# An mLSTM and bilinear layer in one launch: the order of its instructions is planned with other durations, a shared port, other rates of transfers and a model of the clock

## The chip, the cores and the metric

One core of one Trainium2 chip runs the whole program. TensorE is PE here, VectorE DVE, ScalarE ACT, GpSimd POOL, and SyncE, which issues every DMA, SP. The metric is the device time of one execution in microseconds; the shown time is the median of the runs.

## What is computed

An mLSTM over 768 positions for 4 batches and 8 heads of width 40 gives y. Its 3072 rows of 320 then go through a bilinear layer with 1536 hidden columns:

```python
for t in range(S):
    m_new = np.maximum(f + m, i)
    f_stab, i_stab = np.exp(f + m - m_new), np.exp(i - m_new)
    C = f_stab * C + i_stab * outer(v, k)
    n = f_stab * n + i_stab * k
    y = sigmoid(o) * (C @ q) / np.maximum(np.abs(n @ q), 1.0)
x = y as (3072, 320)                    # q, k, v, gates: float32
out = ((x @ w_a) * (x @ w_b)) @ w_out   # w_a, w_b, w_out: float64
```

## The kernel before

The positions are cut into 6 chunks of 128 for each of 4 batches: 24 chunks n, each for all heads. Of a chunk, in this order: `qk` and `va` are loaded; T holds the transposed q (`T<n>_0`) and k (`T<n>_1`); `pS` = k q; the masked weights of the gates are in `gbc<n>` (POOL masks them by affine_select, ACT takes eight exponentials, one for each head, from chunk 4 on); DVE multiplies `pS` with `gbc`; `pI` is q times the state of the chunks before; `pV` is the weighted sum of v; `pU` adds `vw` (v weighed by POOL with columns of `gtab`) times k to the state `cst`; `num`, `den` and `osig` make y; `pX` transposes y into `xh` (cast by ACT) and its rest `xl` (subtracted by DVE). Chunks from 6 on split their operands into bf16 parts: `r`, the `qks` tiles, and `pb`, `vr`, `vl`, `cr`, `cb`.

The columns of all gates, `gtab`, are transposed once (`ptg`), and exponentiated once on ACT, in a table of functions other than that of the sigmoid that makes `osig`.

The 24 chunks are grouped into 9 blocks of 2 or 3 for the bilinear layer. For each ff of 12, `pu<block>_<ff>_0` and `_1` are 8 matmuls each (xh and xl with the high and low parts of w_a and w_b); ACT or DVE copies the first into `g`, DVE multiplies the second into it, `gh` and `gl` are its two parts, and two ff later `pd<block>_<chunk>` gets three matmuls of each chunk. While block kb runs, the chunks of block kb+1 go through the attention, so their instructions lie between those of the block.

The float64 weights come in 32 pieces (`raw0` to `raw31`) and are converted on chip, one after the other, during blocks 0 and 1: two ACT steps (into `qks`, used as scratch, and `cw`), one DVE step on `cw`, a cast `w` on ACT and its rest `w` on DVE. A piece must be done before the matmuls that read it.

No instruction is issued where it is written. Every call goes into a `Plan`, which keeps for each node its engine, a duration `occ`, a delay `lat` until others see it, and its dependences; buffers are rings, so the first user of a slot depends on the last of the tile before. `settle` then lists the nodes: `run` takes, engine by engine, the ready node with the best rank, and ranks are found by running the plan backwards, 6 turns. Nodes that are marked as pinned (the start up to the first weights) keep their written order on an engine. The best plan's order is written out engine by engine, and semaphores keep the dependences on the chip. `HOP` is what a signal between engines takes. The instructions written by `emit` all have the line of its call.

Of the kernel before, what the change touches and what calls it, by code (L numbers as in the profile page):

```python
# [21 lines left out]
TURNS = 6  # L22
LANES = 8


# [74 lines left out]
class Node:  # L100
    __slots__ = (
        "i", "eng", "calls", "occ", "lat", "prev", "next", "table", "acc", "pinned", "at", "done", "xfer",
    )

    def __init__(self, i, eng):
        self.i, self.eng, self.calls, self.prev, self.next = i, eng, [], {}, []
        self.occ = self.lat = self.xfer = 0.0
        self.table, self.acc, self.pinned = None, [], False


class Plan:

    ENGINES = {"tensor": "PE", "vector": "DVE", "scalar": "ACT", "gpsimd": "POOL", "sync": "SP"}
    HOP = 0.07

    def __init__(self, nc):
        self.nc, self.nodes, self.rings, self.pinned = nc, [], {}, True
        for name in self.ENGINES:  # L120
            setattr(self, name, Recorder(self, name))

    def pool(self, pool, space, bufs):
        return Pool(self, pool, space, bufs)

    def add(self, engine, op, args, kw):
        eng = self.ENGINES[engine]
# [12 lines left out]
        if not (  # L140
            eng == "PE" and node is not None and node.eng == "PE" and node.acc[0][0] == okey
            and len(node.calls) < 8 and node.pinned == self.pinned
        ):
            node = Node(len(self.nodes), eng)
            node.pinned = self.pinned
            self.nodes.append(node)
        node.calls.append((engine, op, args, kw))
        node.acc += acc
        self.cost(node, eng, op, out, refs, args, kw)
        return Issued()  # L150
# [15 lines left out]

    def cost(self, node, eng, op, out, refs, args, kw):
        cols = int(np.prod(out.shape[1:]))
        size = [x.size if isinstance(x, View) else mybir.dt.size(x.dtype) for x in refs]
        if eng == "PE":  # L170
# [12 lines left out]
        elif eng == "ACT":  # L183
            func = str(args[2]) if op == "activation" else "Copy"
            node.table = "S" if "Sigmoid" in func else "E" if "Exp" in func else None
            bias = hasattr(kw.get("bias"), "shape")
            node.occ = 0.04 + cols * 0.00094 + (0.13 if bias else 0.0)
            node.occ += 0.05 if "Prelu" in func or "scale" in kw else 0.0
            node.lat = 0.11
        elif eng == "DVE":  # L190
            rate = 960.0
            one = op in ("tensor_copy", "tensor_scalar", "memset") and all(
                not isinstance(x, View) or x.root.ring[0] != "psum" for x in refs
            )
# [4 lines left out]
            node.occ = 0.065 + cols / rate  # L199
            node.lat = 0.085  # L200
        elif eng == "POOL":
            node.occ = 0.1 + cols * (0.0009 if op in ("affine_select", "memset") else 0.002)
            node.lat = 0.1
        elif op == "dma_start_transpose":
            node.occ, node.lat, node.xfer = 1.3, 1.6, 0.0
        else:
            n = int(np.prod(out.shape)) * size[0]
            rows = out.shape[-1] * size[0]
            node.occ, node.lat = 0.47 if rows > 512 else 0.6, 1.7
            node.xfer = n / (340e3 if rows > 512 else 172e3)  # L210

# [35 lines left out]
    def edge(self, a, b, order=False):  # L247
        if a is b or (order and a.i in b.prev):
            return
        if a.eng == b.eng and a.eng != "SP":  # L250
            gap = a.occ
            if a.eng in ("DVE", "ACT", "POOL") and not order:
                gap += 0.06
        else:
            gap = a.occ if order else None
        if order and a.eng != b.eng:
            gap = 0.0
        if a.i not in b.prev:
            a.next.append(b)
            b.prev[a.i] = gap  # L260
        elif gap is None or (b.prev[a.i] is not None and gap > b.prev[a.i]):
            b.prev[a.i] = gap

    def run(self, rank, forward=True):
        nodes = self.nodes
# [6 lines left out]
        end = [0.0] * len(nodes)  # L272
        table, wire, landed = "E", 0.0, []
        order = []
        for x in nodes:
            if lack[x.i] == 0:
                heapq.heappush(wait[x.eng], (0.0, rank[x.i], x.i))
        while len(order) < len(nodes):
            best = None
            for e in engines:  # L280
                if ready[e]:
                    t = free[e]
                elif wait[e]:
                    t = max(free[e], wait[e][0][0])
                else:
                    continue
                if best is None or t < best[0]:
                    best = (t, e)
            t, e = best
            while wait[e] and wait[e][0][0] <= t + 1e-9:  # L290
                r, k, i = heapq.heappop(wait[e])
                heapq.heappush(ready[e], (k, i))
            k, i = heapq.heappop(ready[e])
            x = nodes[i]
            if x.table and x.table != table:
                table = x.table
                t += 1.283
            at[i] = t
            free[e] = t + x.occ
            if e == "SP":  # L300
                if forward:
                    if len(landed) >= LANES:
                        t = max(t, landed[-LANES])
                    at[i], free[e] = t, t + x.occ
                    wire = max(wire, t + x.lat) + x.xfer if x.xfer else wire
                    end[i] = wire + 0.35 if x.xfer else t + x.occ + x.lat
                    landed.append(end[i])
                else:
                    free[e] = t + max(x.occ, x.xfer)
                    end[i] = t + x.occ + x.lat + x.xfer  # L310
            else:
                end[i] = t + x.occ + x.lat
            order.append(x)
            for y in x.next if forward else [nodes[j] for j in x.prev]:
                lack[y.i] -= 1
                if lack[y.i] == 0:
                    r = 0.0
                    if forward:
                        for j, gap in y.prev.items():
                            r = max(r, end[j] + self.HOP if gap is None else at[j] + gap)  # L320
                    else:
                        for z in y.next:
                            gap = z.prev[y.i]
                            r = max(r, at[z.i] + z.occ + (y.lat + self.HOP if gap is None else gap - y.occ))
                    heapq.heappush(wait[y.eng], (r, rank[y.i], y.i))
        return order, at, max(end)

    def settle(self):
# [3 lines left out]
        for turn in range(TURNS):  # L332
            order, at, end = self.run(rank)
            if best is None or end < best[1]:
                best = (order, end, at)
            back, late, _ = self.run([-t for t in at], forward=False)
            rank = [-(t + x.occ) for t, x in zip(late, self.nodes)]
        self.at = best[2]
# [3 lines left out]
    def emit(self, order):  # L342
# [3 lines left out]
        for node in order:  # L346
            for engine, op, args, kw in node.calls:
                f = getattr(getattr(self.nc, engine), op)
                f(*[real(x) for x in args], **{k: real(x) for k, x in kw.items()})  # L349
# [6 lines left out]
class Recorder:  # L356

    def __init__(self, plan, name):
        self._plan, self._name = plan, name

    def __getattr__(self, op):
        return lambda *args, **kw: self._plan.add(self._name, op, args, kw)

# [1058 lines left out]
```

## Time and profile before

| what | value |
|---|---|
| median of 3 runs | 553.07 us (552.47 to 554.78) |
| profiled execution, its own time | 552.61 us |
| its span, first to last instruction | 550.8 us |
| PE busy | 529.5 us, 96% |
| DVE, ACT, POOL busy | 408.0, 234.4, 126.1 us |
| mean granted clock of PE | 0.966 |

Busy time is what an engine works, waits are idle time before an instruction with the one that released it, and the granted clock says which share of the full rate PE had. All rows have line 349, the call in `emit`, so that the names of the tiles tell the steps apart; buffer numbers are left out in the rows, so `T` is any T and `gbc` any gbc.

### The profile page before, as it was taken

The page shows a single profiled execution, that of the slowest core. Times are in us where ns is not written, and L with a number is a line of the kernel's source. Part 1 is how long each engine was busy: PE and PEld are TensorE (multiplying, and loading weights), DVE is VectorE, ACT ScalarE, POOL GpSimd, SP SyncE. Part 2 cuts the span into 40 slices and gives each one's busy share as a digit, 9 for nine tenths or more (in the row PEclk, how much of TensorE's full clock was granted, in tenths as well). Part 3 has the DMA queues.
Part 4 walks back from the last instruction along what each step waited for, and adds up shares of the span by engine and source line. Part 5 has one row for each costly group of instructions (what it writes and reads, how often), then busy time and mean ns, then how long its engine had stood idle before and what let it go on. Part 6 is the DMA issues. An engine that isn't in the chain of part 4 may idle for free. (4 is left out here: it accounts for less than half of the span.)

```text
span 550.8 us, 12384 instructions
## 1 busy us (share of the span) xinstructions
PE 529.5 (96%) x4810; PEld 506.3 (92%) x4810; DVE 408.0 (74%) x940; ACT 234.4 (43%) x556; POOL 126.1 (23%) x185
## 2 busy tenths in 40 slices
PE   7787899989999999999999999999999999999997
PEld 5676899989999999999899999999999999999997
DVE  5897875578969985987869985988869856844342
ACT  5689997354523642432623444432432622311111
POOL 2012353453232231242132131232030202000000
PEclk9668799989999999999999999999999999999999
DMA  9999923559767756479745659567635535100001
GB/s 170 304 255 312 163 54 65 150 87 166 149 142 125 159 121 149 96 123 171 134 118 129 100 131 191 91 137 147 120 107 86 115 64 116 38 1 26 1 1 37
DMA packets 198679, 66.77 MB, mean 121 GB/s; under 512 B 184252, under 2 KB 191900, under 8 KB 198620
## 3 DMA queue, kind: packets, MB, share of 16 engines
q1 hardware_dynamic: 198620, 65.98, 58.1%
q8 instruction: 38, 0.62, 0.5%
q14 instruction: 21, 0.17, 0.1%
HBM read 41.11 MB, written 5.97 MB: 85 GB/s over the span
## 5 line engine op out<-in xcount | busy, mean ns | idle before, releaser
L349 PE MATMUL pu<-xh,w 128*128 128x384 f32 (+1 forms) x1080 | 281.5, 328 | 0.6 <-ACT xh L349 0.6
L349 PE MATMUL pu<-xl,w 128*128 128x384 f32 (+1 forms) x648 | 211.9, 329 | 1.0 <-DVE xl L349 1.0
L349 PEld LDWEIGHTS pu<-xh,w 128*128 128x128 f32 x1080 | 195.6, 194 | 1.7 <-ACT xh L349 1.0
L349 PE MATMUL pd<-w,gh 128*128 128x320 f32 x576 | 134.5, 315 | 0.0
L349 PEld LDWEIGHTS pu<-xl,w 128*128 128x128 f32 x648 | 126.0, 194 | 2.1 <-DVE xl L349 1.3
L349 PEld LDWEIGHTS pd<-w,gh 128*128 128x128 f32 x576 | 98.0, 190 | 0.4
L349 DVE TENSOR_TENSOR g<-pu,g 128x384 f32<-128x384 f32 (+1 forms) x108 | 54.7, 507 | 57.9 <-PE pu L349 53.5
L349 PE MATMUL pd<-w,gl 128*128 128x320 f32 x288 | 90.4, 315 | 0.0
L349 ACT COPY g<-pu 128x384 f32<-128x384 f32 (+1 forms) x92 | 40.3, 438 | 96.5 <-PE pu L349 96.3
L349 ACT ACTIVATE gbc<-gbc,gtab 128x128 f32<-128x128 f32 x160 | 54.3, 394 | 20.5 <-POOL gbc L349 20.5
L349 POOL TENSOR_TENSOR vr<-va 128x336 f32<-128x336 f32 x18 | 14.5, 804 | 211.7 <-PE pV L349 211.7
L349 PEld LDWEIGHTS pd<-w,gl 128*128 128x128 f32 x288 | 54.3, 189 | 0.2 <-DVE gl L349 0.2
L349 DVE TENSOR_TENSOR gl<-g,gh 128x384 fp32r<-128x384 f32 (+1 forms) x92 | 51.7, 562 | 1.9
L349 ACT CAST pb<-gbc 128x512 bf16<-128x512 f32 x36 | 22.3, 619 | 45.0 <-DVE gbc L349 44.8
L349 PE MATMUL pV<-va,gbc 128*128 128x42 bf16 (+1 forms) x240 | 36.2, 235 | 1.8 <-ACT T L349 1.8
L349 DVE CAST gh<-g 128x384 fp32r<-128x384 f32 (+1 forms) x96 | 33.9, 353 | 1.7
L349 DVE TENSOR_TENSOR num<-pV,num 128x336 f32<-128x336 f32 x20 | 10.1, 505 | 32.9 <-PE pV L349 32.9
L349 DVE TENSOR_TENSOR gbc<-pS,gbc 128x512 f32<-128x512 f32 x48 | 32.3, 680 | 2.9 <-PE pS L349 2.3
L349 ACT CAST cb<-cst 128x168 bf16<-128x168 f32 x18 | 6.0, 333 | 61.6 <-DVE cst L349 34.2
L349 PE MATMUL pS<-T,T 120*128 120x128 bf16 (+1 forms) x352 | 29.4, 236 | 1.8 <-DVE T L349 1.8
L349 PEld LDWEIGHTS <-T 120*128 120x128 bf16 x576 | 24.7, 97 | 6.4 <-issue 4.1
L349 POOL TENSOR_TENSOR gl<-g,gh 128x256 fp32r<-128x256 f32 x16 | 13.1, 821 | 56.5 <-ACT gh L349 49.7
(102 smaller groups left out, 763.7 us busy)
## 6 DMA issues: line engine op xcount, KB each, us to landing
gbc<-g_dram SPq DMA_DIRECT2D x20, 512.0 KB
qk<-in_q_dram SPq DMA_DIRECT2D x24, 160.0 KB
qk<-in_k_dram SPq DMA_DIRECT2D x24, 160.0 KB
va<-in_v_dram SPq DMA_DIRECT2D x24, 160.0 KB
osig<-in_o_gate_dram SPq DMA_DIRECT2D x24, 160.0 KB
raw<-in_moe_w_out_dram SPq DMA_DIRECT2D x12, 320.0 KB
out_dram<-o SPq DMA_DIRECT2D x24, 160.0 KB
raw<-in_moe_w_a_dram SPq DMA_DIRECT2D x8, 384.0 KB
```

Of the source, the lines that this page charges most:

```text
L349: f(*[real(x) for x in args], **{k: real(x) for k, x in kw.items()})
```

## The change

Only the planner changes. The durations of most kinds of instructions are set anew, as is HOP; a step after another on the same engine that reads its result costs `DEP`. DVE and POOL exclude each other in the plan where both use the SBUF port that they share (`port`). The plan of PE counts the columns and rows that it uses in a window of `SPELL` us, and doubles the duration of matmuls where the window before was used under 0.375. Transfers are slower (305 and 160 KB per us in place of 340 and 172), a long one lands 1.2 us later in the plan, and of those with short rows no more than two are on the way at a time. Nodes may have several engines to choose from (`alts`, `copier`, `adder`), but no call uses that: every instruction keeps its engine, and the instructions of each engine are the same as before. The core of the diff:

```diff
+SPELL = 3.4133
...
-    HOP = 0.07
+    HOP = 0.05
+    DEP = {"DVE": 0.115, "ACT": 0.115, "POOL": 0.11, "PE": 0.0}
...
                 elif "float32r" in f32[0]:
-                    occ = cols / 2400 + 0.011
+                    occ = cols / 2400 + 0.0135
                 else:
-                    occ = 0.108 if refs[1].shape[0] <= 64 else 0.22
-            node.occ += occ
-            node.lat = 0.17
+                    occ = 0.108 if cols > 64 else 0.052
+            by[0] += occ
+            by[1] = 0.17
+            plain = size[1] == 4 and op == "matmul" and "float32r" not in f32[0]
+            node.use += cols * refs[1].shape[0] * (1 + plain) / 128.0 * out.shape[0] / 128.0
...
-            node.occ = 0.1 + cols * (0.0009 if op in ("affine_select", "memset") else 0.002)
-            node.lat = 0.1
+            by[0] = 0.03 + cols * 0.00205
+            if op == "affine_select":
+                by[0] = 0.05 + cols * 0.001
+            elif op == "memset":
+                by[0] = 0.05 + cols * 0.0008
+            by[1] = 0.06
+            by[3] = op != "memset"
...
-            node.xfer = n / (340e3 if rows > 512 else 172e3)
+            by[2] = n / (305e3 if node.wide else 160e3)
...
+            if shared and forward:
+                t = max(t, port[other[e]])
+                port[e] = t + occ - 0.07
+            if e == "PE" and forward:
+                w = int(t / SPELL)
+                if used.get(w - 1, 0.0) < 0.375 * SPELL * 2400:
+                    occ = 2 * occ
+                used[w] = used.get(w, 0.0) + x.use
...
+                    if not x.wide:
+                        if len(slim) > 1:
+                            free[e] = max(free[e], slim[-2] - 0.3)
-                    end[i] = wire + 0.35 if x.xfer else t + x.occ + x.lat
+                    end[i] = wire + (1.2 if x.wide and xfer > 1.0 else 0.35) if xfer else t + occ + lat
```

The order changes most in blocks 0 and 1 (until about 150 us) and a little after. Three places follow.

ACT ahead of the exponential of `gtab`, some 46 to 50 us into the span (w10 to w12, cw and qks are conversion steps of the weights, gh0_2 a part of block 0). Before:

```order
L349 CAST w10_648<-cw_582 128x384
L349 ACTIVATE qks1_87<-raw13_398 128x320
L349 ACTIVATE cw_659<-raw13_398 128x320
L349 CAST w11_667<-cw_616 128x384
L349 CAST gh0_2_676<-g0_2_588 128x256
L349 ACT_TABLE_LOAD
L349 ACTIVATE osig0_218<-osig0_218 128x2x320
L349 ACT_TABLE_LOAD
L349 ACTIVATE gtab_105<-gtab_105 128x5x64
L349 ACTIVATE dec_106<-pdec_687 128x64
L349 CAST w12_706<-cw_639 64x384 x2
```

Now:

```order
L420 ACTIVATE qks1_87<-raw13_388 128x320
L420 ACT_TABLE_LOAD
L420 ACTIVATE osig0_237<-osig0_237 128x2x320
L420 CAST w10_659<-cw_575 128x384
L420 ACT_TABLE_LOAD
L420 ACTIVATE gtab_105<-gtab_105 128x5x64
L420 ACTIVATE dec_106<-pdec_650 128x64
L420 CAST gh0_2_677<-g0_2_583 128x256
L420 CAST w11_682<-cw_607 128x384
L420 ACTIVATE cw_688<-raw13_388 128x320
L420 CAST w12_702<-cw_625 64x384 x2
```

The cast of w11, gh0_2 and the second step on raw13 stood ahead of gtab and now stand behind it; osig0 and its table load come earlier.

PE around `pI5`, the product of chunk 5 with the state before it, in block 1 at 113 to 119 us. Before, from the end of pu1_4_1 and pU5 on:

```order
L349 MATMUL pu1_4_1_1592<-xh1_999,w12_706 128x256
L349 MATMUL pU5_1606<-vw5_1458,qk2_82 64x42 x8
L349 MATMUL pI5_0_1626<-cst1_91,T5_0_1400 128x42 x2
L349 MATMUL pI5_1_1630<-cst1_91,T5_0_1400 128x42 x2
L349 MATMUL pI5_0_1626<-cst1_91,T5_0_1400 128x42
L349 MATMUL pI5_1_1630<-cst1_91,T5_0_1400 128x42
L349 MATMUL pI5_0_1626<-cst1_91,T5_0_1400 128x42
L349 MATMUL pI5_1_1630<-cst1_91,T5_0_1400 128x42
L349 MATMUL pu1_4_1_1592<-xl1_1016,w12_706 128x256
L349 MATMUL pd1_0_1518<-w7_529,gh1_2_1529 128x320 x2
```

Now pU5 stands 26 rows ahead of the first of pI5 (one row of pu1_4_1, the downs of ff 2 and all of pu1_5 follow it); the last of these, and pI5:

```order
L420 MATMUL pu1_5_1_1635<-xl1_1011,w11_682 128x256
L420 MATMUL pu1_5_1_1635<-xh1_1000,w11_682 128x256
L420 MATMUL pu1_5_1_1635<-xh1_1000,w12_702 128x256
L420 MATMUL pu1_5_1_1635<-xl1_1011,w12_702 128x256
L420 MATMUL pd1_0_1521<-w13_733,gh1_3_1565 128x320 x2
L420 MATMUL pd1_0_1521<-w13_733,gl1_3_1571 128x320
L420 MATMUL pd1_1_1529<-w13_733,gh1_3_1565 128x320 x2
L420 MATMUL pd1_1_1529<-w13_733,gl1_3_1571 128x320
L420 MATMUL pI5_0_1661<-cst1_91,T5_0_1386 128x42 x4
L420 MATMUL pu1_6_0_1668<-xh1_1000,w16_793 128x256
L420 MATMUL pu1_6_0_1668<-xl1_1011,w16_793 128x256
```

pI5 moved behind 29 matmuls that stood behind it, and its two halves are no longer interleaved.

POOL ahead of the masking of gbc5 and gbc6 (AFFINE_SELECT), at 104 to 114 us. Before:

```order
L349 TENSOR_TENSOR osig1_1225<-osig1_1225,den4_1447 128x320
L349 TENSOR_TENSOR vw5_1458<-va2_85,gtab_105 128x336
L349 TENSOR_TENSOR cr4_1474<-cst0_90,cb4_1469 128x168
L349 TENSOR_TENSOR gl1_1_1493<-g1_1_1443,gh1_1_1485 128x256
L349 TENSOR_TENSOR cb4_1469<-cr4_1474,cb4_1469 128x168
L349 AFFINE_SELECT gbc5_1429<-gbc5_1429 128x1024
L349 TENSOR_TENSOR qks0_86<-r6_0_1477,qks0_86 128x8x40
L349 TENSOR_TENSOR gl1_2_1539<-g1_2_1506,gh1_2_1529 128x256
L349 TENSOR_TENSOR qks1_87<-r6_1_1515,qks1_87 128x8x40
L349 AFFINE_SELECT gbc6_1445<-gbc6_1445 128x1024
```

Now:

```order
L420 TENSOR_TENSOR vw5_1452<-va2_85,gtab_105 128x336
L420 TENSOR_TENSOR cr4_1465<-cst0_90,cb4_1454 128x168
L420 TENSOR_TENSOR cb4_1454<-cr4_1465,cb4_1454 128x168
L420 TENSOR_TENSOR gl1_1_1490<-g1_1_1448,gh1_1_1479 128x256
L420 TENSOR_TENSOR qks0_86<-r6_0_1470,qks0_86 128x8x40
L420 TENSOR_TENSOR qks1_87<-r6_1_1493,qks1_87 128x8x40
L420 TENSOR_TENSOR osig1_1239<-osig1_1239,den4_1458 128x320
L420 AFFINE_SELECT gbc5_1436<-gbc5_1436 128x1024
L420 TENSOR_TENSOR gl1_2_1554<-g1_2_1503,gh1_2_1532 128x256
L420 TENSOR_TENSOR gl1_3_1571<-g1_3_1526,gh1_3_1565 128x256
L420 AFFINE_SELECT gbc6_1446<-gbc6_1446 128x1024
```

The masking of gbc5 moved behind the two steps on qks of chunk 6 and the one on osig1 of chunk 4.

Further moves that the prediction speaks of: on PE pT2_0 stands ahead of block 0's first matmul, pS2 close to pU0, pX6, pX12 and pX16 later among the matmuls of their blocks; on DVE the copy T2_1 later; on SP the loads of qk2's first half, va0, gbc4 and qk0 earlier, and raw27 and raw28 exchanged.

More of the change, by code (lines that the diff above doesn't have):

```diff
@@ L23 @@
 LANES = 8
+LATE = {}
+SPELL = 3.4133
 class View:
@@ L100, with __init__ @@
 class Node:
[L101 to L108, printed above, removed]
+    __slots__ = ("i", "eng", "alts", "calls", "by", "prev", "next", "table", "acc", "pinned", "wide", "use")
+    def __init__(self, i, alts):
+        self.i, self.alts, self.eng = i, alts, alts[0]
+        self.calls, self.prev, self.next, self.acc = [], {}, [], []
+        self.by = {e: [0.0, 0.0, 0.0, False] for e in alts}
+        self.table, self.pinned, self.wide, self.use = None, False, True, 0.0
 class Plan:
     ENGINES = {"tensor": "PE", "vector": "DVE", "scalar": "ACT", "gpsimd": "POOL", "sync": "SP"}
-    HOP = 0.07
+    NAMES = {v: k for k, v in ENGINES.items()}
+    HOP = 0.05
+    DEP = {"DVE": 0.115, "ACT": 0.115, "POOL": 0.11, "PE": 0.0}
     def __init__(self, nc):
@@ L140, in add @@
         if not (
-            eng == "PE" and node is not None and node.eng == "PE" and node.acc[0][0] == okey
+            alts[0] == "PE" and node is not None and node.eng == "PE" and node.acc[0][0] == okey
             and len(node.calls) < 8 and node.pinned == self.pinned
         ):
-            node = Node(len(self.nodes), eng)
+            node = Node(len(self.nodes), alts)
             node.pinned = self.pinned
             self.nodes.append(node)
-        node.calls.append((engine, op, args, kw))
+        node.calls.append((op, args, kw))
         node.acc += acc
-        self.cost(node, eng, op, out, refs, args, kw)
+        for eng in alts:
+            self.cost(node, node.by[eng], eng, op, out, refs, args, kw)
         return Issued()
@@ L165, in where, with cost @@
         return name, ((p0, p0 + parts), (f0 * size, (f0 + n) * size))
-    def cost(self, node, eng, op, out, refs, args, kw):
+    def cost(self, node, by, eng, op, out, refs, args, kw):
         cols = int(np.prod(out.shape[1:]))
         size = [x.size if isinstance(x, View) else mybir.dt.size(x.dtype) for x in refs]
+        psum = [isinstance(x, View) and x.root.ring[0] == "psum" for x in refs]
         if eng == "PE":
@@ L186, in cost @@
             bias = hasattr(kw.get("bias"), "shape")
-            node.occ = 0.04 + cols * 0.00094 + (0.13 if bias else 0.0)
-            node.occ += 0.05 if "Prelu" in func or "scale" in kw else 0.0
-            node.lat = 0.11
+            by[0] = 0.04 + cols * (0.00084 if any(psum) else 0.00094) + (0.13 if bias else 0.0)
+            by[0] += 0.05 if "Prelu" in func or "scale" in kw else 0.0
+            by[1] = 0.11
         elif eng == "DVE":
             rate = 960.0
-            one = op in ("tensor_copy", "tensor_scalar", "memset") and all(
-                not isinstance(x, View) or x.root.ring[0] != "psum" for x in refs
-            )
+            one = op in ("tensor_copy", "copy", "tensor_scalar", "memset", "tensor_scalar_max") and not any(psum)
             if one:
@@ L198, in cost @@
                 rate = 480.0
-            node.occ = 0.065 + cols / rate
-            node.lat = 0.085
+            by[0] = 0.065 + cols / rate
+            by[1] = 0.085
+            by[3] = (one or len(refs) > 2) and not any(psum)
         elif eng == "POOL":
-            node.occ = 0.1 + cols * (0.0009 if op in ("affine_select", "memset") else 0.002)
-            node.lat = 0.1
+            by[0] = 0.03 + cols * 0.00205
[5 more added lines that the diff above has]
+            by[3] = op != "memset"
         elif op == "dma_start_transpose":
-            node.occ, node.lat, node.xfer = 1.3, 1.6, 0.0
+            by[0], by[1] = 1.3, 1.6
         else:
             n = int(np.prod(out.shape)) * size[0]
-            rows = out.shape[-1] * size[0]
-            node.occ, node.lat = 0.47 if rows > 512 else 0.6, 1.7
-            node.xfer = n / (340e3 if rows > 512 else 172e3)
+            node.wide = out.shape[-1] * size[0] > 512
+            by[0], by[1] = 0.47 if node.wide else 0.6, 1.7
+            by[2] = n / (305e3 if node.wide else 160e3)
     def link(self):
@@ L247, in edge, with gap, run @@
     def edge(self, a, b, order=False):
-        if a is b or (order and a.i in b.prev):
-            return
-        if a.eng == b.eng and a.eng != "SP":
[L251 to L264, printed above, removed]
+        if a is not b:
+            if a.i not in b.prev:
+                a.next.append(b)
+                b.prev[a.i] = not order
+            elif not order:
+                b.prev[a.i] = True
+    def gap(self, a, b, data):
+        occ, lat = a.by[a.eng][0:2]
+        if a.eng == b.eng and a.eng != "SP":
+            return occ + (self.DEP[a.eng] if data else 0.0)
+        if data:
+            return occ + lat + self.HOP
+        return occ if a.eng == b.eng else 0.0
+    def run(self, rank, forward=True, fixed=None):
         nodes = self.nodes
@@ L272, in run, with put @@
         end = [0.0] * len(nodes)
-        table, wire, landed = "E", 0.0, []
-        order = []
+        done = [False] * len(nodes)
+        when = [None] * len(nodes)
+        turn = dict.fromkeys(engines, 0)
+        table, wire, landed, slim, used = "E", 0.0, [], [], {}
+        port = {"DVE": 0.0, "POOL": 0.0}
+        other = {"DVE": "POOL", "POOL": "DVE"}
+        order = []
+        def put(x, r):
+            when[x.i] = r
+            if fixed is None:
+                for e in x.alts if forward else (x.eng,):
+                    late = LATE.get((x.alts, e), 0.0) if forward else 0.0
+                    heapq.heappush(wait[e], (r + late, rank[x.i], x.i))
         for x in nodes:
             if lack[x.i] == 0:
-                heapq.heappush(wait[x.eng], (0.0, rank[x.i], x.i))
+                put(x, 0.0)
         while len(order) < len(nodes):
@@ L280, in run @@
             for e in engines:
[L281 to L284, printed above, removed]
-                else:
-                    continue
+                if fixed is not None:
+                    if turn[e] == len(fixed[e]) or when[fixed[e][turn[e]]] is None:
+                        continue
+                    t = max(free[e], when[fixed[e][turn[e]]])
+                else:
+                    while ready[e] and done[ready[e][0][1]]:
+                        heapq.heappop(ready[e])
+                    while wait[e] and done[wait[e][0][2]]:
+                        heapq.heappop(wait[e])
+                    if ready[e]:
+                        t = free[e]
+                    elif wait[e]:
+                        t = max(free[e], wait[e][0][0])
+                    else:
+                        continue
                 if best is None or t < best[0]:
@@ L289, in run @@
             t, e = best
[L290 to L293, printed above, removed]
-            x = nodes[i]
-            if x.table and x.table != table:
+            if fixed is not None:
+                i = fixed[e][turn[e]]
+                turn[e] += 1
+            else:
+                while wait[e] and wait[e][0][0] <= t + 1e-9:
+                    r, k, i = heapq.heappop(wait[e])
+                    if not done[i]:
+                        heapq.heappush(ready[e], (k, i))
+                k, i = heapq.heappop(ready[e])
+            x = nodes[i]
+            if forward:
+                x.eng = e
+            done[i] = True
+            occ, lat, xfer, shared = x.by[e]
+            if x.table and e == "ACT" and x.table != table:
                 table = x.table
                 t += 1.283
+            if shared and forward:
[6 more added lines that the diff above has]
+                used[w] = used.get(w, 0.0) + x.use
             at[i] = t
-            free[e] = t + x.occ
+            free[e] = t + occ
+            end[i] = t + occ + lat
             if e == "SP":
@@ L318, in run @@
                     if forward:
-                        for j, gap in y.prev.items():
-                            r = max(r, end[j] + self.HOP if gap is None else at[j] + gap)
+                        for j, data in y.prev.items():
+                            z = nodes[j]
+                            if data and not (z.eng == y.alts[0] != "SP" and len(y.alts) == 1):
+                                r = max(r, end[j] + self.HOP)
+                            elif z.eng == "PE" == y.eng:
+                                r = max(r, free["PE"] if z is x else at[j])
+                            else:
+                                r = max(r, at[j] + self.gap(z, y, data))
                     else:
                         for z in y.next:
-                            gap = z.prev[y.i]
-                            r = max(r, at[z.i] + z.occ + (y.lat + self.HOP if gap is None else gap - y.occ))
-                    heapq.heappush(wait[y.eng], (r, rank[y.i], y.i))
+                            occ2 = z.by[z.eng][0]
+                            r = max(r, at[z.i] + occ2 + self.gap(y, z, z.prev[y.i]) - y.by[y.eng][0])
+                    put(y, r)
+        self.ends = end
         return order, at, max(end)
@@ L334, in settle @@
             if best is None or end < best[1]:
-                best = (order, end, at)
+                best = (order, end, at, [x.eng for x in self.nodes])
             back, late, _ = self.run([-t for t in at], forward=False)
-            rank = [-(t + x.occ) for t, x in zip(late, self.nodes)]
+            rank = [-(t + x.by[x.eng][0]) for t, x in zip(late, self.nodes)]
+        for x, e in zip(self.nodes, best[3]):
+            x.eng = e
         self.at = best[2]
@@ L346, in emit @@
         for node in order:
-            for engine, op, args, kw in node.calls:
-                f = getattr(getattr(self.nc, engine), op)
+            engine = getattr(self.nc, self.NAMES[node.eng])
+            for op, args, kw in node.calls:
+                if op == "copy" and node.eng != "ACT":
+                    op = "tensor_copy"
+                f = getattr(engine, op)
                 f(*[real(x) for x in args], **{k: real(x) for k, x in kw.items()})
@@ L356, with __init__ @@
 class Recorder:
[L358 to L359 removed]
+    def __init__(self, plan, *names):
+        self._plan, self._names = plan, names
     def __getattr__(self, op):
[L362 removed]
+        return lambda *args, **kw: self._plan.add(self._names, op, args, kw)
 class Pool:
```

18 lines of the change are left out of this document (10 added, 8 removed).

## The prediction

> **What bounds the kernel now.** I read the page first, then the waits of TensorE (PE), then the windows for its granted clock, then the timeline around each wait.
>
> ```profile
> PE 529.5 (96%) x4810; PEld 506.3 (92%) x4810; DVE 408.0 (74%) x940; ACT 234.4 (43%) x556; POOL 126.1 (23%) x185
> ```
>
> PE is busy for 96% of the span, so only two things can be won by order alone: its idle time, and the time in which its clock was not full. The idle time, by what ended it:
>
> ```profile
> PE pX L349 <- DVE osig L349: 3.1, 3, 2.4
> PE pU L349 <- POOL vw L349: 3.0, 1, 3.0
> PE pI L349 <- DVE gbc L349: 2.3, 1, 2.3
> PE pV L349 <- ACT T L349: 1.8, 1, 1.8
> PE pS L349 <- DVE T L349: 1.8, 1, 1.8
> PE pX L349 <- DVE gbc L349: 0.8, 2, 0.5
> ```
>
> Columns: who waited for whom, us in total, how often, longest. The windows say when the clock was half (after the busy times stand PEclk, the DMA share and GB/s):
>
> ```profile
> 33.60:40.42 6.82, 6.32 (x38) 6.12 (x39) 6.57 (x15) 4.41 (x12) 1.49 (x4) 0.50 1.08 336
> 50.66:57.49 6.83, 6.57 (x57) 6.18 (x58) 5.91 (x11) 6.81 (x19) 2.68 (x4) 0.50 0.96 219
> 64.32:67.73 3.41, 3.41 (x28) 3.17 (x27) 3.01 (x9) 3.11 (x9) 1.44 (x2) 0.50 1.11 178
> 118.93:125.75 6.82, 6.82 (x33) 6.78 (x32) 5.27 (x16) 1.50 (x4) 2.21 (x4) 0.50 1.06 147
> 125.75:547.50 421.75, 420.18 (x3944) 405.73 (x3943) 316.56 (x741) 146.70 (x349) 86.79 (x110) 1.00 0.53 105
> ```
>
> Each half-clock stretch is one or two times 3.41 us long. PE is nearly always busy in them, but does half the work: the last one, 6.82 us, holds 3.41 us of work at full clock. From 125.75 us to the last matmul only 1.57 us of 421.75 are idle. So the span is the early kernel, where PE waits, and then 422 us of a saturated PE, which no order shortens by more than 1.57 us.
>
> **The change part by part.** The instructions of every engine are the same, and each keeps its engine. So there is no added or removed work to price, only places.
>
> *Front, 0 to 83 us.* These are the rows around the longest wait, and the other two waits:
>
> ```profile
> 50.92 1.09 PE L349 MATMUL pU<-vw,qk 128*64 128x42 f32 x16 [3.02 <-POOL vw L349]
> 45.33 0.51 ACT L349 CAST w<-cw 128x384 fp32r<-128x384 f32 x1 [0.97 <-DVE cw L349]
> 45.75 0.40 ACT L349 CAST gh<-g 128x256 fp32r<-128x256 f32 x1
> 46.17 1.28 ACT L349 ACT_TABLE_LOAD   x1
> 49.52 0.47 ACT L349 ACTIVATE gtab<-gtab 128x320 f32<-128x320 f32 x1
> 51.45 0.48 ACT L349 ACTIVATE cw<-raw 128x320 uint32<-128x320 uint32 x1
> 34.10 1.23 PE L349 MATMUL pS<-T,T 40*128 40x128 f32 x8 [1.76 <-DVE T L349]
> 61.43 1.98 PE L349 MATMUL pV<-va,gbc 128*128 128x42 f32 x16 [1.78 <-ACT T L349]
> ```
>
> pU0 needs vw0 from POOL, vw0 needs the exponential of gtab, and on ACT that stood behind two table loads. In the new order of ACT, three steps leave its front: the `cw` of raw13 (0.48), `w11` (0.51, with the 0.97 us that ACT waited for DVE ahead of it) and `gh0_2` (0.40). That is 2.4 us, so pU0 could start about that much earlier. The `w12` cast and all conversion behind it move up less, because the three steps come back right behind `dec`. pS2 moves behind eight more rows of pu0_3 and close to pU0, while pT2_0 is transposed early; the 1.76 us wait is then likely to show up in another place, since the copy T2_1 moves behind `w9` on DVE. The loads behind this move too: on SP qk2's first half is issued ahead of raw8, va0, gbc4 and qk0 come earlier, and raw27 and raw28 swap. I give these nothing, as the converting engine is what is short here:
>
> ```profile
> 41.00:55.00 14.00, 10.97 (x97) 9.50 (x96) 10.37 (x21) 12.93 (x29) 3.36 (x4) 0.85 1.04 309
> 55.00:69.00 14.00, 12.22 (x109) 11.35 (x105) 11.52 (x24) 13.59 (x35) 5.14 (x9) 0.79 1.08 164
> 69.00:83.00 14.00, 14.00 (x117) 13.48 (x116) 10.28 (x24) 12.78 (x36) 7.39 (x9) 1.00 0.28 53
> ```
>
> ACT (the fourth busy time) works 39.30 of these 42 us. Its work is unchanged, so a start that is earlier by 2.4 us can be kept only as far as ACT's idle 2.70 us shrink; what PE gains at pU0 it may wait again at pV2 or pV3 for a copy on ACT. If the lead is lost wholly the front gives 0; if the whole of pU0's wait is kept, 3.0. I take 1.5, the middle, because ACT has no slack to turn all of it into progress.
>
> *Block 1, the wait at pI5.*
>
> ```profile
> 116.78 1.65 PE L349 MATMUL pI<-cst,T 40*128 40x42 f32 x16 [2.29 <-DVE gbc L349]
> 113.82 0.67 PE L349 MATMUL pU<-vw,qk 128*64 128x42 f32 x16
> 109.31 1.10 POOL L349 TENSOR_SCALAR_AFFINE_SELECT gbc<-gbc 128x1024 f32<-128x1024 f32 x1
> 114.56 2.15 ACT L349 ACTIVATE gbc<-gbc,gtab 128x128 f32<-128x128 f32 x7 [2.27 <-POOL gbc L349]
> 113.01 0.28 PE L349 MATMUL pu<-xl,w 128*128 128x256 f32 x1
> 113.13 0.40 PE L349 MATMUL pu<-xh,w 128*128 128x256 f32 x2
> 126.65 0.46 PE L349 MATMUL pd<-w,gh 128*128 128x320 f32 x2
> 126.94 0.31 PE L349 MATMUL pd<-w,gl 128*128 128x320 f32 x1
> ```
>
> pI5 takes the slot that pS5 leaves when DVE has multiplied it with gbc5, and gbc5's eight exponentials on ACT were interleaved with gbc6's, which stood still for 2.27 us until POOL had masked gbc6. Before, pI5 stood directly behind pU5. Now 29 matmuls stand between: 17 of pu, which start 0.12 apart (113.01, 113.13), are 2.04 us, and 12 of pd at 0.147 (two in 126.65 to 126.94) are 1.76 us. This is 3.80 us of cover against a wait of 2.29, and PE reaches pI5 at 113.82 + 0.67 + 3.80 = 118.3.
>
> When is the slot free? On POOL the masking of gbc5 moves behind three steps that stood behind it or apart from it:
>
> ```profile
> 110.37 1.03 POOL L349 TENSOR_TENSOR qks<-r,qks 128x320 bf16<-128x320 f32 x1
> 112.59 0.80 POOL L349 TENSOR_TENSOR qks<-r,qks 128x320 bf16<-128x320 f32 x1
> 104.55 0.72 POOL L349 TENSOR_TENSOR osig<-osig,den 128x320 f32<-128x320 f32 x1 [2.48 <-DVE den L349]
> 116.62 0.35 ACT L349 COPY g<-pu 128x256 f32<-128x256 f32 x1
> 117.17 0.44 ACT L349 CAST qks<-qk 128x320 bf16<-128x320 f32 x1
> 115.94 1.29 DVE L349 TENSOR_TENSOR gbc<-pS,gbc 128x512 f32<-128x512 f32 x2 [0.55 <-ACT gbc L349]
> ```
>
> So it starts 1.03 + 0.80 + 0.72 = 2.55 us later than 109.31 and ends at 112.96. Seven exponentials at 2.15 / 7 = 0.31 are 2.15; among them stand a g copy (0.35), a copy of osig (as much at most), the cast of qks (0.44) and three exponentials of gbc6 (0.92). That makes 117.2, and one multiplication of 0.65 makes 117.8: 0.5 us ahead of PE. The wait of 2.29 goes, with little to spare.
>
> With it, I expect, goes the half clock behind it, which began 2.15 us after the wait ended: 3.41 us. No row shows what the clock would do without the gap, so this term lies between 0 and 3.41; I take it nearly whole, because in the 422 us that follow, where all gaps together are 1.57 us, the clock is never half. Together 2.29 + 3.41 = 5.70; I take 5.2.
>
> Here the Trainium skill, "TensorE: Matmul & The Clock Gate", section "What's actually happening", speaks against me: it gives half clock after at least one idle window of about 3.4 us. This trace has it after a gap of 2.29 us, so the row decides; by the page the gap would not be the cause, only 2.29 would be won here, and the time would be 3.4 us more than my sum.
>
> *Late waits.* In the waits list pX's 3.1 for osig holds the 2.4 of the front, which stays, and 0.7 at pX12; with the 0.8 for gbc at pX6 and pX16 the late ones are 1.5 us, as the 1.57 idle after 125.75 also says. pX6 moves from the middle of pu1_10 to the downs of ff 10, pX12 behind three downs and the 16 ups of pu3_11, pX16 behind three downs. Each gains 0.4 us of cover or more where under 0.6 was missing. But block 2 reads the xl that comes of pX6, and only three downs, pV7, three downs and pU7 remain ahead of its first matmul.
>
> ```profile
> L349 PE MATMUL pV<-va,pb x16: 180/182/195, 154.9 to 156.0; 128*128 128x42 bf16 x16
> ```
>
> This is one chunk's pV: its first and last matmul start 1.1 us apart. So 6 x 0.147 + 1.2 + 0.67 = 2.75 us must hold a copy on ACT and a subtraction on DVE, about 0.5 us each (the cast of 384 columns at 45.33 took 0.51). I take 0.9 for this part, bounds 0 and 1.57.
>
> **Sum.** 1.5 + 5.2 + 0.9 = 7.6 us. The profiled execution took 552.61 us (span 550.8 and 1.8 around it), so 545.0; the median of the runs, 553.07, lies 0.46 above it, so 545.5.
>
> **The rivals.**
>
> *The clock does not recover.* If it is the many small matmuls of pU5 and pI5 that pull the clock down, and not the gap, the stretch at half clock stays: 545.5 + 3.4 = 548.9. If the front's lead is lost as well, 550.4. For it: at 64.32 the clock goes half behind a gap of only 1.78 us and a row of small matmuls (pV, 1.98 us). Against: there a gap stands ahead too. Chance 0.20.
>
> *The front keeps everything.* pU0's 3.0 us and the half-clock stretch at 64.32 (1.7 us of loss) are both won: 3.2 us below my sum, 542.3. For it: the three steps that leave ACT's front hold 2.4 of the 3.0 us. Against: ACT is 94% busy behind it (39.30 of 42). Chance 0.10.
>
> *Nothing is left of it.* PE is 96% busy; the waits change place and come back at pS2, pV3 or pX6, as the stretched orders of DVE and ACT allow. 550.3 to 555.8. Chance 0.09.
>
> *Slower: the masking of gbc5 comes too late.* It now stands behind qks of r6_1 and osig of den4, and both wait for DVE. DVE's rows stretch where POOL works beside it:
>
> ```profile
> 114.54 0.85 DVE L349 CAST gh<-g 128x256 fp32r<-128x256 f32 x1
> 119.68 0.29 DVE L349 CAST gh<-g 128x256 fp32r<-128x256 f32 x1
> ```
>
> The margin is 0.5 us; from 2.8 us of extra delay on, pI5 waits longer than before, 2.3 us and the 3.4 of the clock are there again, and everything in chunk 6 (its pX6 stands ahead of block 2 with only 2.75 us of cover) is late by the same amount: another wait of 2 to 3 us with its own half-clock stretch of 3.4. With no gain in front that gives 553 + 2.5 + 3.4 - 1 (the two later waits), about 558. Against it: five such stretched steps (0.56 more each) would be needed. Chance 0.08.
>
> The Trainium skill, "SBUF — State Buffer", section "SBUF: two separate sides", calls the port pair of DVE and POOL an exclusive lock; the two rows agree with it, and it makes this rival likelier, not my sum larger.
>
> **How the numbers follow.** My own case (542.5 to 548.5) has 0.53. With 0.20, 0.10, 0.09 and 0.08 that is 1. A difference under 0.5%, 2.8 us, can hardly be told from none, so faster is below 550.3: 0.53 + 0.20 + 0.10 = 0.83; same 0.09; slower 0.08. The largest gain by the bounds is 3.0 + 5.7 + 1.57, which is 542.8, and 1.7 less with the clock of the front: 541.1; with 2 in 10 to be left out I end the range at 541.5. Above, it takes in the clock rival with a lost front and a little of the "nothing left" case: 551.0.
>
> **What would show it.** In the new profile PE's wait at pI should be under 0.8 us and the clock full from about 70 us on; if the wait is gone and half clock remains near 120, the first rival holds. pU's wait should be under 1 us and pV2, which ends its wait at 61.43 now, earlier by 1 to 2 us; if pU is early but pV2 or pV3 waits 2 us or more for ACT, the front gives nothing. pX's waits after 100 us should be under 0.7 us in sum. The prediction is wrong if DVE ends a new wait of over 2 us on PE between 100 and 160 us.

## The result, and the profile after

The median went from 555.37 us (552.47 to 557.14, 8 runs) to 549.85 (547.5 to 550.95, 8 runs): ratio 0.9893, 95% interval 0.986 to 0.9926, so 5.9 us faster (4.1 to 7.8). The ratio is not the quotient of the two medians, which differ by 5.5 us. Forecast were 545.5 us and a gain of 7.6. When both kernels ran again later, the ratio was 0.9893 again (0.9854 to 0.9932).

The two traces must be read with care. The profiled execution before (552.61 us) was one of its fastest, the one after (550.95, span 549.2) the slowest of its 8 runs, so the traces differ by 1.7 us where the medians differ by 5.5. The runs of one kernel differ in how many half-clock windows they catch: the run of 547.5 us had a mean clock of 0.975, the one of 550.86 had 0.966. So the traces show where time went, and the ratios say how much.

The page's engine row, the waits of PE (who waited for whom, us in total, times, longest) and the windows (busy time by engine, then PEclk, DMA share, GB/s) of the changed kernel:

```profile
PE 529.2 (96%) x4810; PEld 506.5 (92%) x4810; DVE 405.6 (74%) x940; ACT 235.6 (43%) x556; POOL 127.5 (23%) x185
```

```profile
PE pV L420 <- ACT T L420: 3.0, 1, 3.0
PE warm L420 <- DVE idle L420: 2.9, 1, 2.9
PE pX L420 <- DVE osig L420: 2.7, 1, 2.7
PE pE L420 <- DVE g L420: 1.4, 1, 1.4
PE pT L420 <- DMA qk<-in_q_dram: 1.3, 1, 1.3
PE pI L420 <- DVE gbc L420: 1.0, 1, 1.0
```

```profile
34.21:41.04 6.83, 5.93 (x27) 5.93 (x28) 6.17 (x14) 6.78 (x18) 2.29 (x5) 0.50 1.00 342
47.86:54.69 6.83, 6.83 (x52) 5.61 (x52) 4.98 (x10) 5.05 (x14) 1.84 (x4) 0.50 1.04 253
54.69:61.52 6.83, 3.70 (x43) 3.12 (x43) 6.77 (x11) 6.02 (x16) 3.54 (x3) 1.00 1.01 254
61.52:64.93 3.41, 3.35 (x16) 3.35 (x16) 2.61 (x5) 2.91 (x8) 0.00 (x0) 0.50 0.83 167
64.93:68.34 3.41, 3.41 (x27) 3.02 (x26) 1.40 (x5) 3.08 (x8) 1.43 (x2) 0.50 0.86 143
68.34:71.76 3.42, 3.42 (x16) 3.42 (x17) 2.98 (x7) 2.31 (x8) 0.00 (x0) 0.50 0.41 44
71.76:545.92 474.16, 472.19 (x4387) 457.08 (x4386) 350.09 (x825) 181.09 (x437) 112.86 (x147) 1.00 0.53 105
```

Gone are the waits of pU0, of pI5 and of the late pX, and the half clock at 118.93 to 125.75: from 71.76 us on the clock is full and PE idles 1.97 us of 474. What is new stands in front. pV2 waits 3.01 us, starts at the same time as before (61.58, before 61.43), and behind it the clock is half for three windows of 3.41 us (61.52 to 71.76), where it was half for one. Over the whole front there are ten such windows in this trace and nine in that of before. By the order of the `pu` matmuls, the first of block 1 starts at 100.18 us, before at 96.90. All of the traces' gain, and more, was made behind that point. pI5, moved behind the 29 matmuls, now starts without a wait:

```profile
121.61 1.08 PE L420 MATMUL pI<-cst,T 40*128 40x42 f32 x8
```

The wait of pV2 in the timeline, PE and then ACT:

```profile
61.58 3.64 PE L420 MATMUL pV<-va,gbc 128*128 128x42 f32 x16 [3.01 <-ACT T L420]
```

```profile
60.53 0.51 ACT L420 CAST w<-cw 128x384 fp32r<-128x384 f32 x1 [0.81 <-DVE cw L420]
60.95 0.58 ACT L420 COPY T<-pT 128x512 f32<-128x512 f32 x1
```

pT3_0, whose slot pV2 takes, was written by 56.06. Its copy on ACT started at 60.95, behind nine steps of weights and a wait of 0.81 us for DVE.

### The profile page after: what moved, and what is told of

Its sections match the earlier page's. It is cut to its first block, busy times and chain, and to the rows that moved or that the text cites. A ratio compares the mean times of both kernels' runs of the same rounds, so it can differ in the third digit from the quotient of the medians.

```text
span 549.2 us, 12389 instructions
## 1 busy us (share of the span) xinstructions
PE 529.2 (96%) x4810; PEld 506.5 (92%) x4810; DVE 405.6 (74%) x940; ACT 235.6 (43%) x556; POOL 127.5 (23%) x185
## 4 chain that ended last, share of the span: by engine, by line
PE 89%; DVE 6%; ACT 3%; issue 1%; POOL 0%; DVEq 0%; ACTq 0%; POOLq 0%
PE pu L420 49%; PE pd L420 23%; PE pV L420 6%; PE pS L420 4%; PE pU L420 2%; PE pI L420 2%; PE pX L420 1%; DVE cw L420 1%; ACT w L420 1%; PE warm L420 1%; PE pT L420 1%; PE pE L420 1%; ACT qks L420 1%; DVE osig L420 1%; DVE g L420 1%
## 5 line engine op out<-in xcount | busy, mean ns | idle before, releaser
L420 DVE CAST gh<-g 128x384 fp32r<-128x384 f32 (+1 forms) x96 | 37.4, 390 | 1.3
L420 POOL TENSOR_TENSOR osig<-osig,den 128x320 f32<-128x320 f32 x22 | 17.3, 785 | 44.4 <-DVE den L420 36.6
L420 ACT CAST qks<-qk 128x320 bf16<-128x320 f32 x36 | 16.4, 455 | 24.2 <-DMA T<-qks 22.5
```

## The experiments

### Which part of the order does it

The list of all instructions in planned order can be cut: one order up to the first matmul of block 1 or 3, then all that is left in the order of the other. `BEFORE` is the list of the kernel before.

```diff
-        return best[0]
+        now, then = [x.i for x in best[0]], BEFORE
+        return splice(now, "pu1_0_0", then)             # front_new
+        return splice(then, "pu1_0_0", now)             # front_old
+        return splice(splice(then, "pu1_0_0", now), "pu3_0_0", then)   # mid_new
```

> The new order up to the first matmul of block 1 (pu1_0_0), the order before from there on. Theory of the prediction: the front alone is worth 1.5 us, so 1.5 us less than before (ratio 0.997). Rival, from the profile after, where block 1 starts 3.27 us later than before because PE waits 3.01 us at pV2 and its clock is half in three windows there: about 3.3 us more than before (ratio 1.006). If the windows fall differently from run to run, the spread is several us and the ratio is near 1.

Measured: 556.83 us against 554.69, ratio 1.0024 (0.9995 to 1.0053).

> The order before up to pu1_0_0, the new order from there on. Theory of the prediction: pI5's wait, its half clock and the late waits are worth 6.1 us (ratio 0.989). Rival: the front costs 3.3 us, so without it the rest shows the whole: about 9 us less than before (ratio 0.984), and less time than the changed kernel.

Measured: 548.86 us, ratio 0.9882 (0.9847 to 0.9918).

> The order before up to pu1_0_0, the new order from there to the first matmul of block 3 (pu3_0_0), the order before again after that. It separates block 1 and 2 from the late waits. Theory of the prediction: 5.2 us less than before (ratio 0.991), and 0.9 more than the kernel with the new order to the end. Rival, from the profile after: the late waits alone are worth 1.4 us and block 2 has a new wait of 1.03 at pI8, so 3 to 4 us less than before.

Measured: 550.46 us, ratio 0.9929 (0.9903 to 0.9956).

The new front gains nothing: by the interval it lies between 0.3 us of gain and 2.9 of loss, and so not at the 1.5 us of gain. The rest alone makes 6.5 us (4.5 to 8.5), as forecast (6.1); the 9 us of the rival lie just outside. Blocks 1 and 2 are 3.9 of it (2.4 to 5.4). The late part would be the 2.6 between the last two, a difference that these intervals hardly tell from 0; the trace of mid_new has late waits of 1.10 us where that of front_old has none, so the waits explain some 1.1.

The forecast of 5.2 for blocks 1 and 2 lies inside the interval too. Where the middle value is less, the trace of the changed kernel shows a reason: pI5's wait is gone, but new ones stand at the end of block 1 and in block 2. From 138 us to 260 PE idles 0.42 + 1.56 us:

```profile
138.00:151.00 13.00, 12.58 (x185) 11.98 (x183) 11.76 (x27) 6.45 (x18) 4.63 (x6) 1.00 0.73 160
151.00:260.00 109.00, 107.44 (x1061) 102.75 (x1060) 93.53 (x223) 43.20 (x106) 31.91 (x40) 1.00 0.77 146
```

Before, the second of these had none, the first 0.47. The waits are 0.42 and 0.38 at two matmuls of pd, 0.14 at a pU, all ahead of block 2's first matmul at 153.40, and the longest is pI8's for gbc8 on DVE:

```profile
169.30 0.56 PE L420 MATMUL pI<-cx,T 120*128 120x42 bf16 x16 [1.03 <-DVE gbc L420]
```

In the trace of mid_new the new waits are 1.75 us. The waits of pI5 (2.29) and pX6 (0.47) and the loss at half clock (3.41) less these are 4.4 us, an estimate from the traces that fits the 3.9 measured.

### Why the front gives nothing

```diff
-        return best[0]
+        # t3_early: the copy of T3_0 on ACT right behind the copy of cst2
+        # t3_both: and the copy of T3_1 on DVE right behind pT3_1 in the list
+        return moved(best[0], T3_0, after=cst2)
```

> The changed kernel with one step moved: the copy of T3_0 on ACT stands right behind the copy of cst2 instead of ten steps later. Theory that pV2's wait of 3.01 us and the half clock behind it come from this copy being queued behind weight steps: 3 us less than the changed kernel by the wait, up to 6.4 with two half-clock windows (ratio to before 0.984 to 0.978). Rival of the prediction, that ACT has no slack in the front and the wait only moves to the next step that needs ACT: within 1 us of the changed kernel (ratio about 0.988).

Measured: 547.32 us (546.01 to 547.95), ratio 0.9858 (0.9831 to 0.9886). That is 2.5 us less than the 549.85 of the changed kernel, from another set of runs; by the ratios it is 1.9, and the two intervals overlap. Its timeline on PE:

```profile
57.38 1.88 PE L422 MATMUL pV<-va,gbc 128*128 128x42 f32 x16
59.19 0.67 PE L422 MATMUL pU<-vw,qk 128*64 128x42 f32 x16
62.68 1.32 PE L422 MATMUL pS<-T,T 40*128 40x128 f32 x8 [2.82 <-DVE T L422]
```

pV2 runs at 57.38 with no wait, 4.2 us earlier (1.0 us of it was gained ahead of that, where this trace has three half-clock windows fewer), so this copy's place was the cause of that wait. But a wait of nearly the same size comes back at pS3, this time for DVE's copy of T3_1. By the middle values the result lies between the two expectations; that it is more than nothing is likely, but the times alone don't show it.

> t3_early with the copy of T3_1 on DVE moved as well, two steps ahead, behind its transposition. In t3_early pV2 no longer waits, but pS3 waits 2.82 us for this copy at 62.68. Theory that the front is a chain of copies that queue behind weight steps: another 0.9 us of that wait goes, ratio to before 0.984. Rival, that DVE has no slack there: the wait comes back at the next step, ratio 0.986 as in t3_early.

Measured: 547.0 us (545.72 to 548.27), ratio 0.9828 (0.979 to 0.9866). The wait at pS3 fell to 1.67 us:

```profile
62.66 2.07 PE L424 MATMUL pS<-T,T 40*128 40x128 f32 x8 [1.67 <-DVE T L424]
```

By the medians it is 0.3 us from t3_early, and the two intervals overlap: this can't be told from none.

### What drops the clock

The prediction took the gap ahead of pI5 as the cause of the half clock behind it. The trace of before already speaks against that, in a stretch that the prediction's list of half-clock windows left out: in the window from 13.12 the profile shows no idle PE at all, and half clock follows it. In it stand the small matmuls of pS (40 rows, 128 columns) and pV (128 rows, 42 columns):

```profile
13.12:16.53 3.41, 3.41 (x39) 3.29 (x37) 2.55 (x8) 2.76 (x5) 0.00 (x0) 1.00 1.23 255
16.53:30.18 13.65, 9.65 (x45) 8.49 (x45) 11.03 (x24) 8.81 (x22) 0.00 (x0) 0.50 1.04 269
```

So two kernels fill the gap ahead of pI5 in the order before, with matmuls whose results are not used: large ones, or small ones like pI's.

```diff
         # behind the matmuls of pU5, ahead of pI5
+        for z in range(24):
+            matmul(pU[:, 256:384], w[0:128, 0:128], xh[0:128, 0:128])   # fill_big: 128 rows, 128 columns
+            matmul(pU[:, 256:298], T5_0[0:40], cst1[0:40])              # fill_small: 40 rows, 42 columns, float32
```

> The order before with 24 extra matmuls of 128 rows by 128 columns (results unused) on PE in the gap ahead of pI5, between pU5 and pI5; nothing else moved. They need 1.5 to 2.4 us, so pI5 comes no earlier. If the half clock behind pI5 comes from what PE did in the window before (a gap or small matmuls), it vanishes: no half clock between 115 and 130 us, and 2.2 to 3.4 us less than before (ratio 0.996 to 0.994). If the clock there has another cause, the half clock stays and the time is that of before.

> As fill_big, but the 24 extra matmuls have 40 rows and 42 columns in float32, like those of pI: PE is as busy in the gap, but uses little of its array. If an idle PE is what drops the clock, this is as good as fill_big: no half clock behind pI5, ratio 0.996 to 0.994. If it is the use of the array, small matmuls don't count: half clock behind pI5 as before, ratio 1.000.

Measured: fill_big 553.33 us against 557.27, ratio 0.9953 (0.9922 to 0.9984); fill_small 562.27, ratio 1.0104 (1.0056 to 1.0151). The windows of fill_big, then those of fill_small:

```profile
116.05:119.47 3.42, 3.42 (x37) 3.30 (x37) 1.72 (x4) 3.12 (x11) 2.15 (x3) 1.00 0.70 136
119.47:133.12 13.65, 12.20 (x120) 11.92 (x119) 12.76 (x33) 4.93 (x13) 5.00 (x6) 1.00 1.15 168
```

```profile
116.05:119.47 3.42, 3.42 (x33) 3.42 (x32) 1.29 (x2) 2.83 (x10) 2.00 (x3) 1.00 1.19 100
119.47:133.12 13.65, 13.65 (x70) 13.53 (x70) 7.55 (x21) 2.13 (x6) 4.46 (x6) 0.50 0.71 147
```

In both the profile shows PE busy throughout from pU5 to pI5. With large matmuls the clock stays full; with small ones it is half for four windows, two more than with the plain gap. The opposite case stands later in fill_small: PE is busy for only 1.85 us of a window, with large matmuls, and the clock behind it stays full:

```profile
273.06:276.48 3.42, 1.85 (x12) 1.38 (x12) 3.42 (x9) 3.39 (x7) 0.92 (x1) 1.00 0.28 54
276.48:279.89 3.41, 3.41 (x22) 3.41 (x21) 1.95 (x5) 1.94 (x6) 0.00 (x0) 1.00 1.27 136
```

So it is not the idle time of the profile that drops the clock. What fits all these windows is how much of the array their matmuls use; a gap is then only one way to use little. Which part of that counts was not separated: the two kinds of fillers differ in rows, columns and type (float32 against fp32r) at once. The ends of matmuls in a profile are modelled, too, so that short pauses between small ones could pass as busy: 33 of them lie in the window of 3.42 us, one for each 0.10 us, nearly the 0.12 that a matmul of 256 columns takes.

fill_big also prices the stretch: 2.6 us (0.9 to 4.3), although its fillers took 2.90 us, longer than the gap and than expected, and pI5 came 1.1 us later than before. In fill_small each float32 matmul makes two rows, and the fillers took 6.24 us. That is 3.95 more than the gap that they fill; with two more windows at half clock (up to 3.4 us) it is enough for the loss of 5.8 us (3.1 to 8.4). The fillers of fill_big, then those of fill_small:

```profile
115.09 2.90 PE L438 MATMUL pU<-xh,w 128*128 128x128 f32 x24
114.80 6.24 PE L438 MATMUL pU<-cst,T 40*128 40x42 f32 x48
```

The front fits this: pV2, pU3 and pS3, all small, stand in a row in the changed kernel, and half clock follows the windows from 61.52 and 64.93, though PE was busy for 3.35 and 3.41 us of 3.41. The last run of this kind puts large matmuls there:

```diff
         # t3_both, and behind the matmuls of pU3, ahead of pS3
+        for z in range(14):
+            matmul(pU[:, 256:384], w[0:128, 0:128], xh[0:128, 0:128])
```

> t3_both with 14 extra matmuls of 128 rows by 128 columns (results unused) ahead of pS3, in its remaining wait of 1.67 us. Theory that low use of the array drops the clock: the half clock that follows (61.82 to 68.65 in t3_both) is shorter by one window or two, 1.5 to 3 us less than t3_both (ratio to before 0.980 to 0.977). Rival: the window ahead holds too little else, the clock drops all the same and the extra matmuls cost nothing or up to 1 us (ratio 0.983 to 0.985).

Measured: 546.34 us (544.4 to 550.98), ratio 0.9853 (0.98 to 0.9905). In its profiled execution, the shortest of all (span 542.6 us), the half clock of this place is gone:

```profile
61.00:68.00 7.00, 6.81 (x52) 6.12 (x52) 6.26 (x16) 6.96 (x19) 1.68 (x2) 1.00 1.16 204
68.00:530.00 462.00, 460.37 (x4308) 445.29 (x4307) 345.48 (x819) 179.61 (x434) 113.58 (x147) 1.00 0.53 108
```

The other runs agree in kind: the mean clock of its six is 0.972 to 0.986, that of t3_both's six 0.971 to 0.975. But its times spread over 6.6 us and its interval holds values of both expectations; whether it beats t3_both stays open.

### Which rule of the planner does it

Each of these takes one rule back and lets the planner make its order anew.

```diff
-                    occ = 2 * occ                              # no_clock
-                t = max(t, port[other[e]])                     # no_port
-            by[2] = n / (305e3 if node.wide else 160e3)        # old_rates
+            by[2] = n / (340e3 if node.wide else 172e3)
```

> The changed kernel once more, beside the others of this call. Ratio to before near 0.989, and a spread of some 3 us between its runs, in steps of the half-clock windows.

Measured: 549.92 us (547.62 to 550.77), ratio 0.9893 (0.9854 to 0.9932).

> The changed planner without its clock model (matmuls are never doubled), all else as changed; the order comes out otherwise. If the clock model is what makes the order better, the gain falls to about half (ratio near 0.995) and a half clock behind pI5 or a wait there returns. If the new durations and the port make it, the ratio stays near 0.989 and pI5 has no wait over 1 us.

Measured: 552.24 us, ratio 0.9911 (0.9879 to 0.9943).

> The changed planner with the rates of transfers as before (340 and 172 KB per us). Weights land ahead of their conversion in both profiles, so I expect no loss: ratio 0.989 within 0.3%. If the rates matter, PE or ACT waits for DMA in the front for 1 us or more, and the ratio is 0.993 or above.

Measured: 548.07 us, ratio 0.9869 (0.9817 to 0.9921).

> The changed planner without the exclusion of DVE and POOL at their port. If the port is what makes the order better, steps on DVE come out late on the chip and waits for DVE return on PE: ratio 0.995 or above. If not, 0.989.

Measured: 557.36 us, ratio to before 1.003 (0.999 to 1.007); the changed kernel beside it took 549.92.

Taking back the clock model or the rates of transfers changes nothing that these runs can tell. Without the port the whole gain is gone. The waits and half-clock windows of that kernel:

```profile
PE pI L420 <- DVE gbc L420: 3.7, 3, 2.1
```

```profile
61.71:71.95 10.24, 9.52 (x54) 8.83 (x54) 7.96 (x18) 10.14 (x29) 2.44 (x4) 0.50 0.80 119
123.15:133.39 10.24, 10.24 (x47) 10.16 (x48) 4.28 (x14) 1.77 (x5) 2.48 (x5) 0.50 0.48 114
211.90:215.31 3.41, 3.41 (x15) 3.15 (x14) 3.41 (x8) 2.83 (x9) 0.00 (x0) 0.50 0.95 182
```

The waits that return are those of pI for DVE's gbc, the kind that the change had taken out, and behind two of them the clock is half again for four windows in all. So the forecast of a gain in block 1 was right in what is won there; which rule wins it was not asked in the prediction. The port is needed for it. Whether the port alone would do, without the new durations, was not run. Nor is it shown that planning the steps of DVE and POOL apart is what brings gbc in time, and not a chance of this one order: each rule was taken back once.

## Why the prediction was right or wrong

- *Direction, range.* Right: 549.85 lies in 541.5 to 551.0, and the gain of 5.9 us is 78% of the 7.6. Of the 4.35 us between 545.5 and 549.85, 2.3 are the base, whose median was 553.07 in three runs and 555.37 in eight; the front, 2.8 us off, accounts for the rest.
- *Front, 1.5 us.* This term failed: it was mis-sized, and its middle value has the wrong sign. Measured: a loss of 1.3 us (by the interval, from 0.3 of gain to 2.9 of loss). pU0 lost its wait and starts 1.97 us earlier, pT3 3.09 earlier, as the step says, and the sign named for failure came true: pU early, and 3.01 us of wait at pV2, which starts no earlier. Two reasons in it were wrong. The lead was not lost for want of slack on ACT, which in the changed kernel is less busy than before in the same windows:

```profile
41.00:55.00 14.00, 12.90 (x113) 10.88 (x112) 10.75 (x21) 12.13 (x27) 3.82 (x7) 0.75 1.07 270
55.00:69.00 14.00, 10.80 (x81) 9.84 (x78) 11.17 (x22) 12.13 (x29) 4.98 (x5) 0.73 0.94 202
69.00:83.00 14.00, 14.00 (x106) 13.74 (x106) 9.29 (x23) 11.15 (x32) 2.58 (x4) 0.90 0.18 28
```

  It works 35.41 of the 42 us, not 39.30 (it did more from 28 to 41 us: 12.28 against 10.40); what made the wait was one copy in a late place of its queue, as t3_early shows. And the lower bound of 0 left out that a front with more small matmuls in a row can lose clock. The runs point that way: the mean clock is 0.961 over the 12 runs of front_new and 0.965 over the 21 of before, and one half-clock window (1.7 us of loss) lowers it by 0.003. That this is the front's loss is not shown, as the interval holds 0.
- *pI5, 2.29 us.* Right: no wait there, in front_old neither, where block 1 follows the front of before. The sign named for it, a wait at pI under 0.8 us, was missed by its letter: 1.03, but at pI8.
- *The half clock behind pI5, up to 3.41.* Right in size (fill_big: 0.9 to 4.3 us), and wrong in its reason, so that the size came out by luck. Not the gap as such counts but the little use of the array in that window. The new order moved 29 large matmuls in, so the stretch went either way; the first rival, small matmuls as the cause, was right about the cause and wrong about what the change makes of it. The rule of the Trainium skill that the prediction weighed ("TensorE: Matmul & The Clock Gate", section "What's actually happening": half clock after an idle window of some 3.4 us) does not agree either: fill_small shows half clock behind a window without idle PE in the profile, and the measurement decides.
- *Late waits, 0.9.* Right in kind: those of pX12 and pX16 are gone, 1.10 us, and so is pX6's of 0.47. That they save time is not shown, as front_old and mid_new can hardly be told apart. The prediction put no new waits into its sum: 1.97 us of them came (0.42, 0.38, 0.14 and 1.03).
- *The slower rival* did not come about in this order. In no_port it nearly did: waits of pI for gbc, with half clock behind them.

## What to carry to other kernels

Look for the cause of a wait in the place of one step in its queue, not in the busy share of the engine that runs it: a copy that frees a buffer, queued behind nine steps with no hurry, held PE for 3 us on an engine that had slack. When small matmuls must run, try large ones between them, so that no window of some 3.4 us holds only small ones: in fill_big that paid 2.6 us, in t3_fill it stays open. Tell a planner that orders by costs which engines shut each other out: here nothing was left of the gain of 1.1% without that one rule.

The lowest ratio is that of t3_both, the changed kernel with two copies moved: 0.9828 of the time before (0.979 to 0.9866). Its interval overlaps with those of t3_early and t3_fill.

## What was not expected of the hardware

A PE that the profile shows busy without a break can fall to half clock: 3.42 of 3.42 us busy with matmuls of 40 rows and 42 columns, and then 13.65 us at 0.50, while 24 matmuls of 128 rows by 128 columns in the same place kept it at 1.00. And the windows don't lie at the same times in each run: the same stretch at half clock starts at 34.21 us in one trace of the changed kernel and at 34.02 in the other. So the same kernel catches more or fewer half windows, each worth up to 1.7 us: the mean clocks of the changed kernel's first 8 runs go from 0.966 to 0.975, and their times over 3.5 us. The profiled executions show 10 half windows (changed kernel, both times), 5 (t3_early) and 9 (t3_both); these are three orders, so that not all of this is chance. A kernel with many short stretches of low use is thus noisy by several us, and a single trace against a single trace says little below 1%.
